# Weight tiles grouped 2, 1, 4 and 3, parameter vectors on SyncE's queue, and one transposing load for each of B and C

## The chip, the cores and the metric

The kernel runs on one core of one Trainium2 chip. The metric is device time in microseconds (us), from the start to the end of one execution. A profile is one further execution, taken by the hardware profiler; its span runs from the first to the last instruction of the program.

## What is computed

A layer norm over 2048 rows of 512 features, and then the sum of three things: the input itself, a diagonal state-space model (SSM), and a gated feed-forward block. The state matrix B has 512 states by 512 features, C has 512 features by 512 states, and the feed-forward block is 1376 wide.

```python
xn = layernorm(x)                                   # (1, 2048, 512)
# A: state-space model, one complex state per p
Lam_bar = exp(exp(log_dt) * (Lambda_re + 1j * Lambda_im))
B_bar = ((Lam_bar - 1.0) / Lam)[:, None] * (B_re + 1j * B_im)
Bu = einsum("bld,pd->blp", xn, B_bar)
h[t] = Lam_bar * h[t - 1] + Bu[:, t]                # over 2048 steps
yA = 2.0 * einsum("blp,dp->bld", h, C).real + xn * Dskip
# B: feed-forward block
yB = (silu(xn @ w_gate) * (xn @ w_up)) @ w_down     # width 1376
out = x + yA + yB
```

All inputs are bfloat16.

## The kernel before

The 2048 rows are worked through in four chunks of 512 rows, each of four tiles of 128 rows. `xall` holds the input by row tiles, `xnT` the normalised rows transposed (features on the partitions). The feed-forward width is cut into eleven feature tiles `fi`: ten of 128 and one of 96.

The order of all work is written out by hand. TensorE (PE) carries the matmuls: gate and up products of a feature tile (`gu_mm`, L425: four matmuls of 512 columns for gate and four for up), the products with B (`bproj_tile`, L350: `part` 0 is the real half, `part` 1 the imaginary half; for each part four state tiles `q`, each of four matmuls over the feature blocks `k`), the down product (L505) and the product with C (L514). ScalarE (ACT) empties the accumulators, VectorE (DVE) does the norms and the SSM's scan, GpSimd (POOL) a few small operations and the stores of results that are added to the output.

The head is finer. While the first chunk's rows arrive tile by tile, `head_mm` (L597) multiplies each row tile as it comes with the first three feature tiles (`H = 3`, `fi` 0 to 2), gate (`which` 0) and up (1). `xT_pe(n)` (L213) transposes row tile `n` on PE; with tile 2 it also transposes the twelve parameter rows `prm_rows` (L243), from which DVE and ACT make the SSM's constants. After the head the order on PE is: gate and up of `fi` 3 to 6 (`G0 = 7`), B with chunk 0 (`part` 0, then `part` 1), gate and up of `fi` 7 to 9, the last feature tile, B with chunk 1, and so on.

The loads that feed this go out on three queues, in the order in which the code names them:

- SyncE (SP): `xall` tile 0, gate weights of group 0, `xall` tile 2, gate and up weights of group 1 (L130, L131), the second chunk's rows in two loads of two tiles (L136), gate and up of group 2 (L137, L138), B's real half in four transposing loads (L141), gate and up of group 3, B's imaginary half in four transposing loads, the last feature tile's weights (L146, L147), then the transposes of chunk 1's normalised rows (`xT_dma`, L227), what `load_late` brings, and C in eight transposing loads (L714).
- ACT: `xall` tile 1, up weights of group 0, `xall` tile 3.
- POOL: the three parameter vectors (L134), 1 KB each, ahead of the identity matrix that PE's transposes need and of an index ramp.

A group is a run of feature tiles that one load brings for gate and one for up, given by `fgroups`: (0, 2), (2, 4), (4, 7), (7, 10) before. A load's line in the profile is L112, the body of `load_w1`.

In the built program, loads from SP and ACT take eight semaphores in turn, and a load is issued only when the load that last used its semaphore, the eighth before it in the order of the code, has landed. A reader of the data waits on the same semaphore, so it waits for a whole load: for one block `k` of B with four loads, for a whole half of B with one.

Of the kernel before, what the change touches and what calls it, by code (L numbers as in the profile page):

```python
# [23 lines left out]
def kernel(  # L24
# [17 lines left out]
    nc = tc.nc  # L42
# [8 lines left out]
    TPC = CW // 128  # L51
    KD = D // 128
    NQ = Pst // 128
    FT = (F + 127) // 128
# [24 lines left out]
    x_v = A_x[0].rearrange("(n p) d -> p n d", p=128)  # L79
# [5 lines left out]
    xall = const.tile([128, NT, D], BF16, name="xall")  # L85
    xnT = const.tile([128, KD, L], BF16, name="xnT")

    fgroups = [(0, 2), (2, 4), (4, 7), (7, FT - 1)]
    wg_g, wu_g = [], []
    for gi, (a, b) in enumerate(fgroups):  # L90
        cols = min(F, b * 128) - a * 128
# [5 lines left out]
    BT = const.tile([128, 2, KD, Pst], BF16, name="BT")  # L97
    CT = const.tile([128, 2, NQ, D], BF16, name="CT")
# [11 lines left out]
    def load_w1(q, tiles, view, gi):  # L110
        a, b = fgroups[gi]
        q.dma_start(out=tiles[gi][:], in_=view[:, :, a * 128:min(F, b * 128)])  # L112
# [18 lines left out]
    load_w1(nc.sync, wu_g, wu_v, 1)  # L131
    prm_rows = const.tile([3 * NQ, 128], BF16, name="prm_rows")
    for i, v in enumerate((A_Lambda_re, A_Lambda_im, A_log_dt)):
        nc.gpsimd.dma_start(out=prm_rows[i * NQ:(i + 1) * NQ, :], in_=v.rearrange("(q j) -> q j", j=128))  # L134
    for n in (TPC, TPC + 2):
        nc.sync.dma_start(out=xall[:, n:n + 2, :], in_=x_v[:, n:n + 2, :])  # L136
    load_w1(nc.sync, wg_g, wg_v, 2)  # L137
    load_w1(nc.sync, wu_g, wu_v, 2)  # L138
    for part, src in enumerate((A_B_re, A_B_im)):
        for k in range(KD):  # L140
            nc.sync.dma_start_transpose(out=BT[:, part, k, :], in_=src[:, k * 128:(k + 1) * 128])  # L141
        if part == 0:
            load_w1(nc.sync, wg_g, wg_v, 3)
            load_w1(nc.sync, wu_g, wu_v, 3)
# [565 lines left out]
        pump(GU)  # L710
        multiply(1)
    for part, src in enumerate((A_C_re, A_C_im)):
        for q in range(NQ):
            nc.sync.dma_start_transpose(out=CT[:, part, q, :], in_=src[:, q * 128:(q + 1) * 128])  # L714

    bproj_chunk(1)
    fwd1, back1 = ssm_ops(1)
# [52 lines left out]
```

## Time and profile before

| | |
|---|---|
| median of 3 runs | 179.78 us (179.59 to 179.90) |
| the profiled execution | 179.83 us |
| its span | 178.1 us |
| outside the span | 1.7 us |
| PE busy | 173.7 us, 98% of the span |
| DVE, ACT, POOL busy | 153.3, 94.2, 23.2 us |
| granted clock of PE | 0.999 |

The span in 40 slices of 4.45 us, busy share in tenths:

```profile
PE   7899999999999999999999999999999999999993
DVE  3789997999999999999999999999999999940033
ACT  3579696978499966033997660024866610220000
DMA  5998956994236400021920000007286900073012
GB/s 159 327 254 204 144 98 174 361 184 104 44 76 218 180 0 0 0 29 14 137 61 0 0 0 0 4 0 81 29 125 84 156 2 0 0 79 39 4 48 70
```

A digit is the busy share of one slice, 9 for 90% or more; for DMA it is the mean of the core's 16 DMA engines, and the last row is what they moved. PE is at 9 from the third slice to the last but one. The DMA engines are full in the second to fourth slice (4.5 to 18 us), when the first weights, the second chunk's rows and B come in.

### The profile page before, as it was taken

To read this page: it belongs to the slowest core of one execution; us is meant where nothing else is said; L and a number is where in the kernel's file an instruction comes from. 1 tells how busy PE (TensorE), PEld (TensorE's weight loads), DVE (VectorE), ACT (ScalarE), POOL (GpSimd) and SP (SyncE) were. 2 spreads that over 40 slices of the span, in tenths; PEclk is the share of its full clock that TensorE was granted. 3 is DMA by queue.
4 is the path that set the end of the run, shared out by engine and by line. 5 is a ranking of instruction groups with operands and counts; after the bars stand their busy time and mean duration, and the time that the engine had idled before them with its cause. 6 is when DMAs were issued, how large, how long until landed. Compare 5 with 4: busy or idle time off the path is not lost.

```text
span 178.1 us, 2462 instructions
## 1 busy us (share of the span) xinstructions
PE 173.7 (98%) x916; PEld 83.2 (47%) x916; DVE 153.3 (86%) x233; ACT 94.2 (53%) x173; POOL 23.2 (13%) x29
## 2 busy tenths in 40 slices
PE   7899999999999999999999999999999999999993
PEld 2784444444444444444444444444444444444743
DVE  3789997999999999999999999999999999940033
ACT  3579696978499966033997660024866610220000
POOL 6003000001400000029100000013405000150000
PEclk9999999999999999999999999999999999999999
DMA  5998956994236400021920000007286900073012
GB/s 159 327 254 204 144 98 174 361 184 104 44 76 218 180 0 0 0 29 14 137 61 0 0 0 0 4 0 81 29 125 84 156 2 0 0 79 39 4 48 70
DMA packets 29131, 15.53 MB, mean 87 GB/s; under 512 B 17824, under 2 KB 29056, under 8 KB 29088
## 3 DMA queue, kind: packets, MB, share of 16 engines
q1 hardware_dynamic: 24416, 11.41, 28.9%
q0 software_dynamic: 3456, 3.28, 14.5%
q10 hardware_dynamic: 1248, 0.69, 1.4%
q8 instruction: 7, 0.11, 0.3%
q14 instruction: 4, 0.03, 0.1%
HBM read 8.03 MB, written 5.24 MB: 75 GB/s over the span
## 4 chain that ended last, share of the span: by engine, by line
PE 96%; DMA 1%; DVE 1%; issue 0%
PE ps L425 36%; PE ps L505 21%; PE ps L514 16%; PE ps L350 16%; PE ps L597 3%; PE ps L451 2%; DMA xall<-in_A_x_dram 1%; PE ps L461 1%; PE ps L213 1%; DVE stats L178 0%; DVE stats L604 0%; DVE xall L196 0%; DVE res L517 0%; PE ps L574 0%; DVE mv L179 0%
## 5 line engine op out<-in xcount | busy, mean ns | idle before, releaser
L505 PE MATMUL ps<-wd_sb,guT 128*128 128x512 bf16 (+3 forms) x198 | 38.8, 355 | 0.0
L425 PE MATMUL ps<-xnT,wg 128*128 128x512 bf16 x148 | 38.0, 379 | 0.0
L425 PE MATMUL ps<-xnT,wu 128*128 128x512 bf16 x148 | 38.0, 379 | 0.0
L392 DVE TENSOR_TENSOR_SCAN g<-r_t,car,u 128x512 bf16<-128x512 f32 x24 | 28.9, 1265 | 0.0
L514 PE MATMUL ps<-CF,wt 128*128 128x512 bf16 (+2 forms) x144 | 28.3, 355 | 0.0
L350 PE MATMUL ps<-xnT,BT 128*128 128x512 bf16 x128 | 28.3, 379 | 0.0
L505 PEld LDWEIGHTS <-guT 128*128 128x128 bf16 (+1 forms) x198 | 18.5, 98 | 19.9
L521 ACT CAST res<-ps 128x512 bf16<-128x512 f32 x12 | 7.0, 585 | 38.5 <-PE ps L514 38.5
L439 ACT ACTIVATE guT<-ps 128x512 bf16<-128x512 f32 x40 | 24.8, 619 | 3.9 <-PE ps L425 3.7
L440 ACT CAST u<-ps 128x512 bf16<-128x512 f32 x40 | 24.2, 604 | 4.2 <-PE ps L425 4.2
L425 PEld LDWEIGHTS <-wu 128*128 128x128 bf16 x148 | 14.5, 98 | 17.5
L425 PEld LDWEIGHTS <-wg 128*128 128x128 bf16 x148 | 14.3, 98 | 17.6 <-issue 0.8
L522 POOL DMA_DIRECT2D out_dram<-res x12 | 11.1, 997 | 87.2 <-ACT res L521 87.2
L514 PEld LDWEIGHTS <-wt 128*128 128x128 bf16 x144 | 13.4, 98 | 14.3
L350 PEld LDWEIGHTS <-BT 128*128 128x128 bf16 x128 | 12.5, 98 | 15.1
L352 ACT CAST u<-ps 128x512 bf16<-128x512 f32 x32 | 17.5, 589 | 3.1 <-PE ps L350 3.1
L517 DVE TENSOR_TENSOR res<-ps,xn_end 128x512 bf16<-128x512 f32 (+2 forms) x6 | 3.0, 514 | 14.6 <-PE ps L514 14.6
L444 DVE TENSOR_TENSOR guT<-guT,u 128x1024 bf16<-128x1024 bf16 x20 | 13.5, 680 | 0.0
L178 DVE BATCH_NORM_STATS2 stats<-xall 128x6 f32<-128x512 bf16 x14 | 9.4, 670 | 1.9 <-DMA xall<-in_A_x_dram 1.9
L360 DVE TENSOR_TENSOR pm<-u,c 128x2048 bf16<-128x2048 bf16 x8 | 9.8, 1220 | 1.2 <-ACT c L277 1.1
L188 POOL TENSOR_TENSOR rstd<-ve,neg_half 128x4 f32<-128x4 f32 x3 | 5.3, 1750 | 40.7 <-DVE ve L187 40.7
L360 DVE TENSOR_TENSOR pm<-g,c 128x2048 bf16<-128x2048 bf16 x8 | 9.7, 1218 | 0.1
(103 smaller groups left out, 156.9 us busy)
## 6 DMA issues: line engine op xcount, KB each, us to landing
out_dram<-in_A_x_dram SPq DMA_DIRECT2D x1, 1536.0 KB, 8.0
out_dram<-res POOLq DMA_DIRECT2D x12, 128.0 KB, 3.2
out_dram<-xall POOLq DMA_DIRECT2D x3, 512.0 KB, 5.9
wd_sb<-in_B_w_down_dram SPq DMA_DIRECT2D x1, 1280.0 KB, 10.6
xall<-in_A_x_dram SPq DMA_DIRECT2D x1, 1024.0 KB, 5.9
wg<-in_B_w_gate_dram SPq DMA_DIRECT2D x2, 384.0 KB, 5.4
wu<-in_B_w_up_dram SPq DMA_DIRECT2D x2, 384.0 KB, 6.0
wg<-in_B_w_gate_dram SPq DMA_DIRECT2D x2, 256.0 KB, 4.5
```

The lines of the kernel that those rows point to most:

```text
L178: nc.vector.bn_stats(out=stats[:, n, :], in_=xall[:, n, :])
L350: nc.tensor.matmul(ps[:], lhsT=BT[:, part, k, q * 128:(q + 1) * 128], rhs=xnT[:, k, c * CW:(c + 1) * CW], start=(k == 0), stop=(k == KD - 1))
L352: nc.scalar.copy(out=u_tiles[c][:, part, q, :], in_=ps[:])
L360: V.tensor_tensor(out=t[:], in0=flat(src()[:, i]), in1=flat(tab[:]), op=ALU.mult)
L392: V.tensor_tensor_scan(out=g()[:, part, q, :], data0=r_t[:, q:q + 1].to_broadcast([128, CW]), data1=u_tiles[c][:, part, q, :], initial=ini ...
L425: nc.tensor.matmul(ps[:fs, lo:hi], lhsT=wslice(groups, fi, k), rhs=xnT[:, k, c * CW + lo:c * CW + hi], start=(k == 0), stop=(k == KD - 1))
L439: nc.scalar.activation(out=guT[:fs, fi, :], in_=psg[:fs], func=ACT.Silu)
L440: nc.scalar.copy(out=u_pair[c][:fs, fi % 2, :], in_=psu[:fs])
L444: products.append(lambda: V.tensor_tensor(out=g, in0=g, in1=u, op=ALU.mult))
L505: nc.tensor.matmul(o[:], lhsT=gu_tiles[c][:fsz[fi], fi, i * 128:(i + 1) * 128], rhs=wd_sb[:fsz[fi], fi, lo:hi], start=(fi == 0), stop=False)
L514: nc.tensor.matmul(o[:], lhsT=w_tiles[c][:, part, q, i * 128:(i + 1) * 128], rhs=CF[:, part, q, lo:hi], start=False, stop=(part == 1 and q ...
L522: nc.gpsimd.dma_start(out=out_v[:, n, lo:hi], in_=res[:, lo:hi], accum_op=ALU.add)
```

## The change

Four edits, all of loads; no arithmetic changes.

```diff
-    fgroups = [(0, 2), (2, 4), (4, 7), (7, FT - 1)]
+    fgroups = [(0, 2), (2, 3), (3, 7), (7, FT - 1)]
...
     for i, v in enumerate((A_Lambda_re, A_Lambda_im, A_log_dt)):
-        nc.gpsimd.dma_start(out=prm_rows[i * NQ:(i + 1) * NQ, :], in_=v.rearrange("(q j) -> q j", j=128))
-    for n in (TPC, TPC + 2):
-        nc.sync.dma_start(out=xall[:, n:n + 2, :], in_=x_v[:, n:n + 2, :])
+        nc.sync.dma_start(out=prm_rows[i * NQ:(i + 1) * NQ, :], in_=v.rearrange("(q j) -> q j", j=128))
+    for a, b in ((0, 1), (1, 2), (2, 4)):
+        nc.sync.dma_start(out=xall[:, TPC + a:TPC + b, :], in_=x_v[:, TPC + a:TPC + b, :])
     load_w1(nc.sync, wg_g, wg_v, 2)
     load_w1(nc.sync, wu_g, wu_v, 2)
     for part, src in enumerate((A_B_re, A_B_im)):
-        for k in range(KD):
-            nc.sync.dma_start_transpose(out=BT[:, part, k, :], in_=src[:, k * 128:(k + 1) * 128])
+        nc.sync.dma_start_transpose(out=BT[:, part, :, :], in_=src[:, :])
...
     for part, src in enumerate((A_C_re, A_C_im)):
-        for q in range(NQ):
-            nc.sync.dma_start_transpose(out=CT[:, part, q, :], in_=src[:, q * 128:(q + 1) * 128])
+        nc.sync.dma_start_transpose(out=CT[:, part, :, :], in_=src[:, :])
```

Group 1 shrinks from two feature tiles to one (256 KB to 128 KB for gate, the same for up), and group 2 grows from three to four (384 KB to 512 KB each): feature tile 3 moves from group 1 to group 2. The three parameter loads stand on SP behind the up weights of group 1. The second chunk's rows come in loads of one, one and two tiles. Each half of B and of C, 512 KB, comes in one transposing load in place of four of 128 KB. SP then issues four transposing loads of B and C in place of sixteen, three parameter loads and one row load more; its order is otherwise the same, and the instructions of PE, DVE and ACT stand in the same order as before.

## Prediction, on record before the changed kernel ran

> **What bounds the kernel now.** I read the chain of waits first (it says which engine sets the end), then the waits of TensorE (PE), then the weight loads of PE in the head, SyncE's (SP's) queue in time order, and last the loads of short windows with their time to landing.
>
> The chain of waits, by engine, and the list of everything PE waited for:
>
> ```profile
> PE 96%; DMA 1%; DVE 1%; issue 0%
> PE ps L574 <- PEq L754: 0.8, 1, 0.8
> PE ps L213 <- DVE xall L196: 0.7, 1, 0.7
> ```
>
> From 4.96 us PE never waits as long as the view lists. So the end comes where the sum of PE's work puts it: a gain must come from small gaps in the head, and a load that comes late costs its lateness in full, because nothing later has slack to give back.
>
> The small gaps, in PE's weight loads (start, duration, in brackets the idle time before and what ended it):
>
> ```profile
> 7.44 0.27 PEld L597 LDWEIGHTS <-wu 128*128 128x128 bf16 x4
> 7.88 0.33 PEld L597 LDWEIGHTS <-wg 128*128 128x128 bf16 x4 [0.18 <-DMA wg<-in_B_w_gate_dram]
> 8.23 0.32 PEld L213 LDWEIGHTS <-xall 128*128 128x128 bf16 x4
> 8.65 0.09 PEld L243 LDWEIGHTS <-prm_rows 12*128 12x128 bf16 x1
> 8.78 0.33 PEld L597 LDWEIGHTS <-wu 128*128 128x128 bf16 x4
> 12.08 0.58 PEld L425 LDWEIGHTS <-wg 128*128 128x128 bf16 x4
> 12.78 0.53 PEld L425 LDWEIGHTS <-wu 128*128 128x128 bf16 x3
> ```
>
> At 7.88 the gate weights of feature tile 2 (group 1) come 0.17 us late: PE's matmuls stood 0.056 apart up to 7.66, and the next started at 7.89. At 8.78 the up weights (landed at 8.74) are up to 0.07 late. Feature tile 3 starts at 12.08 (gate) and needs its up weights at 12.78; tile 3 is what moves into the later, larger group.
>
> SP's issues (start, us):
>
> ```profile
> 2.20 0.43 SPq L112 DMA_DIRECT2D wg<-in_B_w_gate_dram  x1
> 2.67 0.51 SPq L112 DMA_DIRECT2D wu<-in_B_w_up_dram  x1
> 3.23 1.71 SPq L136 DMA_DIRECT2D xall<-in_A_x_dram  x2
> 4.98 0.47 SPq L112 DMA_DIRECT2D wg<-in_B_w_gate_dram  x1
> 5.81 0.87 SPq L112 DMA_DIRECT2D wu<-in_B_w_up_dram  x1
> 6.72 6.26 SPq L141 DMA_TRANSPOSE BT<-in_A_B_re_dram  x4
> 13.03 1.24 SPq L112 DMA_DIRECT2D wg<-in_B_w_gate_dram  x1
> 14.86 5.36 SPq L141 DMA_TRANSPOSE BT<-in_A_B_im_dram  x4
> ```
>
> A plain load costs SP about 0.5 us, a transposing one of 128 KB about 1.26. Adding the times to landing (5.6, 6.1, 6.3, 5.7, 6.4 and 6.8 us in the trace for group 1's gate and up, the two row loads, group 2's gate and up) gives landings at 7.84, 8.74, 9.49, 10.25, 11.43 and 12.62: in order of issue, each later than the one before by its own size. So the queue is the limit there, and prices are differences: 256 KB in 512-byte rows 0.90 us, 256 KB of x in 1024-byte rows 0.755, 384 KB in 768-byte rows 1.185. B's halves landed at 15.90 and 22.30 (last load of each: issue at 11.72 plus 4.2, at 18.96 plus 3.3); PE starts on B here:
>
> ```profile
> 19.04 7.07 PE L350 MATMUL ps<-xnT,BT 128*128 128x512 bf16 x32
> ```
>
> Sixteen of these 32 matmuls, 0.216 us apart, belong to the real half, so the imaginary half is first needed at 19.04 + 16 x 0.216 = 22.49.
>
> **The change part by part.**
>
> *Group 1 smaller.* Rows of 128 columns are 256 bytes, which no plain load of the trace has. Per row (32 on each of 16 DMA engines) the prices above are 28.1 ns for 512 bytes, 37.0 for 768 and 47.2 for 1024: a line with 9 ns at its foot, so 18.6 ns for 256 bytes and 0.60 us for a load. Bounds: 0.45 (half of 0.90) and 0.90. I take 0.60, as three rows lie on the line. Group 1's gate then lands at 7.84 - 0.30 = 7.54, its up weights at 8.14. PE wants them at 7.66 and 8.65 or sooner. The gain is 0.17 + 0.04 (half of the 0.07) = 0.21; bounds 0 and 0.35 (with the 0.10 that PE loses ahead of L243, whose cause the trace doesn't tell).
>
> *Parameters on SP.* POOL loses 0.69 + 0.56 + 0.52 us of issues; its identity matrix, done at 3.6, is first used at 4.96 after DVE, so this gives nothing. On SP the three issues (some 0.45 each) wait for the loads eight back, which landed at 2.96, 3.64 and 4.55; the next issue, x, must wait for group 0's up weights at 5.85 in any case, so these issues lie in a wait. The vectors land behind group 1's up weights, at about 8.2; PE needs them at 8.65 - 0.17 = 8.48. Cost 0, by 0.3 us of cover; beyond it each tenth costs a tenth, and DVE's and ACT's constants (L246 to L252) come as much later.
>
> *x in three.* Issues at 5.87, 6.3 and 6.8, landings 8.14 plus 0.38, 0.38 and 0.755: 8.52, 8.90, 9.65. DVE reads them from 11.59. Cost 0. The queue doesn't run dry: the first load of all took 2.2 us alone, so x could land at 8.1 at the earliest, before its turn.
>
> *Group 2 larger.* 512 KB in 1024-byte rows is 2 x 0.755 = 1.51 us. Gate may be issued when group 1's gate has landed (7.54) and lands at 9.65 + 1.51 = 11.16, up at 12.67. PE, 0.21 ahead, wants gate at 11.9 and up at 12.78 - 0.21 = 12.57 for loading ahead, or 12.74 at the latest for a matmul at 12.79. Cost 0, but the cover is 0.1 us: with 0.90 for each load of group 1 up lands at 13.27 and feature tile 3's up matmuls start at 13.32 in place of 13.00, 0.32 later than before.
>
> *B in one load each.* No row has a transposing load of 512 KB. Its issue is bounded by 1.25 us (one of the present ones) and by 7.95 (C's real half, four issues in a full queue, 30.89 to 38.84); between lie 5.0 (4 x 1.26), 5.36 and 6.26. I take 5.0: the work per byte is the same. SP gets to the real half when group 2's up issue is over, at 8.15 + 0.87 = 9.0 (before: 6.72). Real half issued until 14.0, group 3's two loads until 15.0, imaginary half until 20.0. Landing follows the end of an issue by 1.2 us (transposes of chunk 1's rows: 2.4 to landing with 1.22 of issue) to 2.1 (last load of the imaginary half, 3.35 - 1.26). So the real half lands by about 16.1, needed at 18.6; the imaginary half at 21.2 to 22.1. It is needed whole at 22.49 - 0.21 = 22.28, where before the first matmul needed a quarter of it. Cost 0, cover 0.2 to 1.1 us. Behind these on SP are the last tile's weights (needed at 31.3), chunk 1's transposes (issued at 21.51 before, about 21.2 now; needed at 32.15, landed by 27.95) and the late loads: cover of 4 us and more. Group 3 is needed at 25.7 and lands before 20.
>
> A rule bears on this: the Trainium skill, "Advanced Engine Details and Errata", section "X-Bar Transpose (TRN2)", says that transposing DMAs on this chip are as fast as regular ones. The trace disagrees: 1.26 us of SP against 0.5, and 3.3 us from 12.62 to 15.90 for 512 KB. By the rule the imaginary half would land long before it is needed, the sum would be the same, and the first rival below would be gone.
>
> *C in one load each.* First read by ACT at 58.8, landed by 45.5 before: 13 us of cover, cost 0.
>
> *Sum* against the profiled execution: 179.83 - 0.21 = 179.6 us, which is 0.1% under the median of the runs shown (179.78).
>
> **The rivals.**
>
> 1. *The imaginary half of B comes late (slower).* The real half takes 6.26 us of SP again, group 3's gate 1.24, the imaginary half 5.36: 9.0 + 6.26 + 1.24 + 0.6 + 5.36 = 22.5, landing at 23.7 to 24.5. PE then stands 1.4 to 2.3 us at `part` 1, net +1.2 to +2.1: about 181.4. It decides from a landing after 22.3. For it: the cover is thin, SP starts B 2.3 us later, and the present issues did take so long. Against: 1.1 of the 6.26 fell in the first load, at 6.72, with a queue that is shorter by 9.0.
> 2. *The up weights of feature tile 3 come late*: 0.90 for a load of group 1, +0.32: 180.15. Against: three row sizes lie on one line. With a landing 0.1 later still it passes 0.2%.
> 3. *Both of PE's head gaps and the 0.10 ahead of L243 vanish*: -0.35, 179.48.
> 4. *The large transposing load works like four*: then B lands as before and only the head counts; this is within the forecast.
>
> **How the numbers follow.** 0.2% (0.36 us) is about what a measurement of this kernel can tell from no change. Forecast, -0.35 to +0.2 us: 0.50. Rival 1: 0.33, nearly all of it slower. Rival 2: 0.12, half of it over 0.2%. Rival 3 or more: 0.05. A gain over 0.36 us has no gap in PE that could pay for it, so faster gets 0.07, for what I haven't seen; slower 0.33 + 0.06 = 0.39 with rounding up to 0.41; same 0.52. The likeliest time is 179.6. The range runs from 179.4 (rival 3 less 0.1 of scatter between runs) to 181.4 (the middle of rival 1); the forecast's own range is 179.45 to 180.05.
>
> **What would show it.** Right: no PEld wait on a DMA at 7.7 to 8.8; feature tile 3's up weights loaded without a gap at about 12.6; 32 L350 matmuls in 6.9 to 7.1 us without a wait; the chain still 96% PE. Wrong: a PE wait on `wu` near 12.8 or on `BT` near 18.6 or 22.3, or one on `prm_rows` near 8.5; an issue of a transposing load far from 5.0 us.

## The result, and the profile after

The changed kernel takes 180.68 us (median of 7 executions, 180.21 to 181.10) against 179.78 (7 executions, 179.59 to 180.02): ratio 1.0052, 95% interval 1.0035 to 1.0068. It is 0.9 us slower where no change was forecast. The profiled execution took 180.64 us: 178.57 of span and 2.07 outside it, against 178.05 and 1.78.

The chain of waits of the changed kernel, by engine, and further down some of its pieces in order of time (start, duration, what). Lines of code have moved up by one or two:

```profile
PE 91%; DMA 6%; SPq 1%; issue 0%; DVE 0%
```

```profile
6.95 0.43 SPq L136
...
7.42 0.47 SPq L112
...
7.93 5.60 DMA wu<-in_B_w_up_dram
13.53 0.05 issue
13.58 6.22 PE ps L424 x28
19.80 6.91 PE ps L349 x32
```

Before, the chain was 96% PE and 1% DMA. Now it runs over SP's issues to one load, the up weights of group 2, and from 13.58 us on it is PE alone. What PE waited for (total, times, longest):

```profile
PE ps L573 <- PEq L752: 0.8, 1, 0.8
PE ps L424 <- DMA wu<-in_B_w_up_dram: 0.4, 1, 0.4
PE ps L212 <- DVE xall L195: 0.2, 1, 0.2
```

The middle line is new. Its place, in PE's weight loads:

```profile
7.80 0.37 PEld L596 LDWEIGHTS <-wg 128*128 128x128 bf16 x4
8.19 0.32 PEld L212 LDWEIGHTS <-xall 128*128 128x128 bf16 x4
8.61 0.09 PEld L242 LDWEIGHTS <-prm_rows 12*128 12x128 bf16 x1
8.72 0.33 PEld L596 LDWEIGHTS <-wu 128*128 128x128 bf16 x4
...
12.09 0.55 PEld L424 LDWEIGHTS <-wg 128*128 128x128 bf16 x4
13.58 0.55 PEld L424 LDWEIGHTS <-wu 128*128 128x128 bf16 x4 [0.94 <-DMA wu<-in_B_w_up_dram]
```

The gap at feature tile 2's gate weights, 0.18 before, is gone at 7.80. At feature tile 3 the weight loads stand idle for 0.94 us until the up weights have landed. The matmuls there, before and after:

```profile
12.13 1.03 PE L425 MATMUL ps<-xnT,wg 128*128 128x512 bf16 x4
13.00 1.03 PE L425 MATMUL ps<-xnT,wu 128*128 128x512 bf16 x4
```

```profile
12.10 1.04 PE L424 MATMUL ps<-xnT,wg 128*128 128x512 bf16 x4
13.58 1.04 PE L424 MATMUL ps<-xnT,wu 128*128 128x512 bf16 x4 [0.45 <-DMA wu<-in_B_w_up_dram]
```

The up matmuls follow the gate matmuls by 1.48 us in place of 0.87. So the wait holds PE up by 0.61 us (the 0.45 in brackets is shorter because the ends of overlapping matmuls are modelled), and of the gap that was closed only 0.03 us of lead was left here. The up matmuls start 0.58 us later than before; B starts at 19.64 (before 19.04), and the last matmul of all at 175.60 (before 175.01). The +0.58 at 13 us is the +0.59 at the end: nothing later is late, and nothing later gives back. B itself takes what it took:

```profile
19.64 7.07 PE L349 MATMUL ps<-xnT,BT 128*128 128x512 bf16 x32
```

SP's queue shows where the lateness comes from:

```profile
2.68 0.51 SPq L112 DMA_DIRECT2D wu<-in_B_w_up_dram  x1
3.23 0.44 SPq L134 DMA_DIRECT2D prm_rows<-in_A_Lambda_re_dram  x1
4.30 0.26 SPq L134 DMA_DIRECT2D prm_rows<-in_A_Lambda_im_dram  x1
4.60 0.29 SPq L134 DMA_DIRECT2D prm_rows<-in_A_log_dt_dram  x1
6.06 1.31 SPq L136 DMA_DIRECT2D xall<-in_A_x_dram  x3
7.42 0.47 SPq L112 DMA_DIRECT2D wg<-in_B_w_gate_dram  x1
7.93 0.51 SPq L112 DMA_DIRECT2D wu<-in_B_w_up_dram  x1
8.48 4.96 SPq L140 DMA_TRANSPOSE BT<-in_A_B_re_dram  x1
```

The parameter loads have taken three semaphore turns. The rows that were issued at 3.23 are issued from 6.06, and group 2 at 7.42 and 7.93 in place of 4.98 and 5.81. Meanwhile the loads that were in flight land (group 1 at 6.92 and 7.26), and the DMA engines have nothing to do. The changed kernel's windows (stretch, length, busy times with counts, granted clock, DMA share, GB/s):

```profile
5.50:6.50 1.00, 1.00 (x18) 1.00 (x16) 0.92 (x3) 0.41 (x2) 0.00 (x0) 1.00 1.16 266
6.50:7.25 0.75, 0.75 (x17) 0.73 (x14) 0.72 (x3) 0.71 (x3) 0.00 (x0) 1.00 0.08 13
7.25:8.50 1.25, 1.25 (x22) 1.21 (x19) 0.81 (x3) 0.63 (x3) 0.00 (x0) 1.00 0.87 270
8.50:10.00 1.50, 1.50 (x24) 1.33 (x22) 1.12 (x6) 0.42 (x3) 0.00 (x0) 1.00 0.95 244
10.00:11.50 1.50, 1.50 (x31) 1.50 (x28) 1.24 (x9) 1.47 (x2) 0.00 (x0) 1.00 1.03 343
```

For 0.75 us they move 13 GB/s, then 244 to 270 until 10 us, and only then 343. In the kernel before the same stretches were full:

```profile
6.50:7.25 0.75, 0.75 (x16) 0.73 (x14) 0.71 (x3) 0.74 (x3) 0.00 (x0) 1.00 1.12 300
7.25:8.50 1.25, 1.24 (x19) 1.02 (x17) 0.76 (x3) 0.62 (x3) 0.00 (x0) 1.00 1.12 347
8.50:10.00 1.50, 1.50 (x23) 1.31 (x21) 1.08 (x6) 0.28 (x2) 0.00 (x0) 1.00 1.09 332
```

Group 2's up weights land at 13.53; before, with loads a quarter smaller, at 12.62, when feature tile 3 did not yet depend on them.

Outside the span the changed kernel takes 2.08 us (median of its executions) against 1.79 in the kernel before. That is the other part of the loss.

### The profile page after: what moved, and what is told of

Its sections match the earlier page's. It is cut to its first block, busy times and chain, and to the rows that moved or that the text cites. A ratio compares the mean times of both kernels' runs of the same rounds, so it can differ in the third digit from the quotient of the medians.

```text
span 178.6 us, 2437 instructions
## 1 busy us (share of the span) xinstructions
PE 174.4 (98%) x916; PEld 83.4 (47%) x916; DVE 153.2 (86%) x233; ACT 95.2 (53%) x173; POOL 21.4 (12%) x26
## 4 chain that ended last, share of the span: by engine, by line
PE 91%; DMA 6%; SPq 1%; issue 0%; DVE 0%
PE ps L424 36%; PE ps L504 21%; PE ps L513 16%; PE ps L349 15%; DMA wu<-in_B_w_up_dram 3%; DMA wg<-in_B_w_gate_dram 3%; PE ps L450 2%; PE ps L460 1%; SPq L112 0%; SPq L128 0%; SPq L136 0%; SPq L123 0%; DVE res L516 0%
```

## The experiments

For each run the kernel before was run on the same chip beside it (for e1 to e14 15 to 27 executions, medians of 179.69 to 179.90 us, of the span 177.9 to 178.1). "SP" is the number of loads and stores that SP issues, "up lands" the landing of group 2's up weights, "gap" PE's idle time in front of feature tile 3's up matmuls as the profile shows it, "tail" from the last matmul's start to the span's end; these four are from the profiled execution. Span and outside are medians over the executions.

| run | SP | up lands | gap | tail | span | outside | ratio to before, interval |
|---|---|---|---|---|---|---|---|
| before | 50 | 12.62 | 0 | 3.04 | 178.0 | 1.79 | |
| after | 42 | 13.53 | 0.45 | 2.96 | 178.6 | 2.08 | 1.0052 [1.0035, 1.0068] |
| e1 | 39 | 12.29 | 0 | 3.20 | 178.15 | 1.81 | 1.0004 [0.9993, 1.0014] |
| e2 | 42 | 12.97 | 0 | 2.96 | 178.2 | 2.01 | 1.0017 [1.0007, 1.0027] |
| e3 | 54 | 13.47 | 0.35 | 3.74 | 179.65 | 1.78 | 1.0084 [1.0059, 1.0109] |
| e4 | 53 | 12.44 | 0 | 3.85 | 178.85 | 1.79 | 1.0044 [1.0027, 1.0061] |
| e5 | 42 | 11.43 | 0 | 2.97 | 178.0 | 2.08 | 1.0016 [1.0006, 1.0025] |
| e6 | 41 | 13.45 | 0.27 | 3.05 | 178.9 | 1.94 | 1.0064 [1.0042, 1.0087] |
| e7 | 50 | 12.27 | 0 | 2.99 | 177.9 | 1.77 | 0.9998 [0.9988, 1.0008] |
| e8 | 42 | 13.03 | 0 | 2.92 | 178.35 | 2.06 | 1.0043 [1.0028, 1.0058] |
| e9 | 50 | 12.68 | 0 | 3.04 | 178.2 | 1.78 | 1.0007 [0.9999, 1.0016] |
| e10 | 38 | 12.45 | 0 | 3.27 | 178.15 | 1.80 | 1.0012 [1.0003, 1.0021] |
| e11 | 50 | 13.53 | 0.19 | 3.03 | 179.0 | 1.77 | 1.0066 [1.0037, 1.0095] |
| e12 | 42 | 12.35 | 0 | 3.00 | 177.95 | 2.19 | 1.0022 [1.0011, 1.0033] |
| e13 | 47 | 12.76 | 0 | 3.17 | 178.25 | 1.79 | 1.0016 [1.0007, 1.0025] |
| e14 | 50 | 11.43 | 0 | 3.06 | 178.0 | 1.77 | 1.0001 [0.9992, 1.0010] |

Theory A: the parameter loads' three semaphore turns delay the rows and group 2, the queue runs empty, and the up weights of feature tile 3, which the new groups have put into the later load, come late. Its rivals put the wait down to the size of group 2's loads (theory B), or to the single transposing loads (theory C).

**e1: the parameters back on POOL**, all the rest of the change kept.

```diff
-        nc.sync.dma_start(out=prm_rows[i * NQ:(i + 1) * NQ, :], in_=v.rearrange("(q j) -> q j", j=128))
+        nc.gpsimd.dma_start(out=prm_rows[i * NQ:(i + 1) * NQ, :], in_=v.rearrange("(q j) -> q j", j=128))
```

> The changed kernel with the parameter loads back on POOL. Theory A (semaphore turns): the three parameter loads and the extra row load push the second chunk's rows and group 2 four turns back, so they are issued at 6.06 and later in place of 3.23, the DMA engines stand idle from 6.5 to 7.25 us, and feature tile 3's up weights land at 13.53. Without the parameter loads x goes out at 3.2 again, up lands by 12.7, PE's wait of 0.9 us at its weight load goes, and the span is 178.0 or less (0.5 to 0.6 below the changed kernel's 178.6). Theory B (size): the 512 KB group is late by itself; the wait at feature tile 3 stays at 0.4 us or more and the span at 178.5. Outside the span: 1.7 us (as before) if POOL's loads decide it, 2.05 (as changed) if they don't.

The rows and group 2 go out as soon as in the kernel before, and the wait is gone. SP's queue of this run, and then its windows:

```profile
3.22 2.27 SPq L136 DMA_DIRECT2D xall<-in_A_x_dram  x3
5.97 0.38 SPq L112 DMA_DIRECT2D wg<-in_B_w_gate_dram  x1
6.43 0.47 SPq L112 DMA_DIRECT2D wu<-in_B_w_up_dram  x1
```

```profile
6.50:7.25 0.75, 0.75 (x14) 0.75 (x13) 0.57 (x3) 0.27 (x1) 0.00 (x0) 1.00 1.17 274
7.25:8.50 1.25, 1.25 (x23) 1.21 (x21) 0.89 (x3) 0.78 (x4) 0.00 (x0) 1.00 1.10 338
8.50:10.00 1.50, 1.50 (x20) 1.30 (x19) 1.00 (x6) 0.51 (x3) 0.00 (x0) 1.00 1.07 343
```

The DMA engines are full where they stood still. With the same 512 KB loads of group 2 and the same single transposing loads, the up weights land 1.24 us sooner (12.29), and the time is that of the kernel before. (The span of this run's one profile, 178.6, is long for another reason, slow matmuls in the head, see the end; the median over the executions is 178.15.)

**e2: the old groups**, all the rest of the change kept.

```diff
-    fgroups = [(0, 2), (2, 3), (3, 7), (7, FT - 1)]
+    fgroups = [(0, 2), (2, 4), (4, 7), (7, FT - 1)]
```

> The changed kernel with the old groups 2, 2, 3, 3. Theory A and B alike: feature tile 3 lies in group 1 again and has landed by 9, so PE has no wait near 13; feature tile 4 needs group 2 at 13.65 and 14.5, where up lands at about 13.4. Span about 178.0 to 178.2. Theory C (the transposing loads slow the weights or B itself comes late): a wait stays, span 178.5. Outside the span: 2.05 if the groups have no part in it.

No wait either: group 2 is late here too (12.97), but feature tile 3 is in group 1. So the wait takes both edits. What is left of the ratio, 1.0017, is for the most part the time outside the span (2.01).

**e3: B and C in four transposing loads each again**, all the rest of the change kept.

```diff
-        nc.sync.dma_start_transpose(out=BT[:, part, :, :], in_=src[:, :])
+        for k in range(KD):
+            nc.sync.dma_start_transpose(out=BT[:, part, k, :], in_=src[:, k * 128:(k + 1) * 128])
```

(The same for C.)

> The changed kernel with four transposing loads for each half of B and of C. Theory A and B: nothing changes for feature tile 3, its up weights land at about 13.5 and the span stays at 178.4 to 178.8. Theory C (the one long issue from 8.48 us slows the 1024-byte packets of group 2, which took 0.2 to 0.7 us each at 8.4 to 9.8): group 2 lands 0.5 us or more earlier, span 178.1. Outside the span: 1.7 if the number of transposing loads decides it, else 2.05.

The up weights land at 13.47, the wait stays: theory C, by which B's single load holds them up, falls. (Its expectation reads slow packets off the changed kernel's trace; they are a few among many, see the next part.) The run is slower still, because the tail behind the last matmul grew to 3.74 us.

**e4: the parameters on SP alone**, the kernel before otherwise.

```diff
-        nc.gpsimd.dma_start(out=prm_rows[i * NQ:(i + 1) * NQ, :], in_=v.rearrange("(q j) -> q j", j=128))
+        nc.sync.dma_start(out=prm_rows[i * NQ:(i + 1) * NQ, :], in_=v.rearrange("(q j) -> q j", j=128))
```

> The kernel before with only the parameter loads moved to SP. Theory A: x goes out at about 6 in place of 3.23 and group 2 about 2 us later, but feature tile 3 lies in group 1, so PE waits little: span within 0.2 of 178.1. If the parameters came late PE would wait at L243 near 8.6. Outside the span: 2.05 if moving POOL's loads decides it, else 1.7.

No wait at feature tile 3, and the last matmul starts at 174.89, a little earlier than before. The whole loss is in the tail: 3.85 us in place of 3.04. It is not what slows the changed kernel, whose tail is 2.96; e9 and e10 ask for its cause.

**e5: group 2 ahead of the second chunk's rows**, in the changed kernel.

```diff
+    load_w1(nc.sync, wg_g, wg_v, 2)
+    load_w1(nc.sync, wu_g, wu_v, 2)
     for a, b in ((0, 1), (1, 2), (2, 4)):
         nc.sync.dma_start(out=xall[:, TPC + a:TPC + b, :], in_=x_v[:, TPC + a:TPC + b, :])
-    load_w1(nc.sync, wg_g, wg_v, 2)
-    load_w1(nc.sync, wu_g, wu_v, 2)
```

> The changed kernel with the two loads of group 2 issued ahead of the three of the second chunk's rows. Theory A (the up weights of feature tile 3 come late because the parameter loads take three semaphore turns, so that SP issues the rows and group 2 at 6.06 to 8.4 us in place of 3.2 to 6.7, and the DMA engines stand nearly idle from 6.5 to 7.25): group 2 is issued at about 6.0 and 6.5, its up weights land at 10.5 to 11.5 us instead of 13.53, PE has no wait on them at feature tile 3, and the span's median comes down from 178.6 to 178.0 to 178.2; with the 2.05 us outside the span, which nothing here should change, 180.1 to 180.3. Rival (the load of four feature tiles is itself slow): a wait on the up weights stays, and so does 180.6.

As theory A has it. SP's queue of this run, and its weight loads at feature tile 3:

```profile
4.75 0.29 SPq L134 DMA_DIRECT2D prm_rows<-in_A_log_dt_dram  x1
5.93 0.39 SPq L112 DMA_DIRECT2D wg<-in_B_w_gate_dram  x1
6.37 0.51 SPq L112 DMA_DIRECT2D wu<-in_B_w_up_dram  x1
7.10 1.52 SPq L138 DMA_DIRECT2D xall<-in_A_x_dram  x3
```

```profile
12.14 0.59 PEld L424 LDWEIGHTS <-wg 128*128 128x128 bf16 x4
12.84 0.74 PEld L424 LDWEIGHTS <-wu 128*128 128x128 bf16 x4
```

The queue still runs empty (44 GB/s from 6.50 to 7.25), but what goes out first is now what PE wants first. The span is back at 178.0; the 2.08 outside stays.

**e6: the rows in two loads**, in the changed kernel: one turn fewer.

```diff
-    for a, b in ((0, 1), (1, 2), (2, 4)):
-        nc.sync.dma_start(out=xall[:, TPC + a:TPC + b, :], in_=x_v[:, TPC + a:TPC + b, :])
+    for n in (TPC, TPC + 2):
+        nc.sync.dma_start(out=xall[:, n:n + 2, :], in_=x_v[:, n:n + 2, :])
```

> The changed kernel with the second chunk's rows in two loads of two tiles, as before: one semaphore turn fewer in front of group 2. Theory A: gate of group 2 waits for one load less and is issued about 0.5 us earlier, the up weights land at about 13.0 in place of 13.53, PE's wait there shrinks from 0.6 to about 0.1 us: span about 178.1 to 178.3. If the three row loads cost nothing, as predicted, the landing stays at 13.5 and the span at 178.6.

A miss for my expectation. Group 2's loads are issued 0.5 to 0.6 us earlier (6.90 and 7.32), as expected, and yet the up weights land at 13.45, not 13.0. So it isn't the issue of the last load that sets the landing. Nor is it the point at which the queue starts again: the first rows were issued at 5.69 here and at 6.06 in the changed kernel, and all rows had landed at 9.22 and at 9.66, but here the gate weights took 2.84 us behind them. What counted was how slowly the engines then worked: from 8.50 to 10.00 they moved 219 GB/s (244 in the changed kernel). The third row load costs nothing, as predicted.

**e7: the new groups alone**, in the kernel before.

```diff
-    fgroups = [(0, 2), (2, 4), (4, 7), (7, FT - 1)]
+    fgroups = [(0, 2), (2, 3), (3, 7), (7, FT - 1)]
```

> The kernel before with the new groups alone: parameters stay on POOL, rows in two loads, B and C in four loads for each half. The prediction's own terms: the wait of 0.17 us at feature tile 2's gate weights goes, group 2's up weights land at about 12.5 to 12.7, with no wait on them: span 0.1 to 0.25 us under the 178.1 of the kernel before, nothing changed outside it, 179.6 to 179.75. Rival (group 2 with four tiles is too big to land in time in any arrangement): a wait on the up weights near 12.8 and 180.0 or more.

With a full queue 512 KB are no trouble: the up weights land at 12.27, and PE doesn't wait. Its weight loads at feature tile 2:

```profile
7.54 0.27 PEld L597 LDWEIGHTS <-wu 128*128 128x128 bf16 x4
7.76 0.37 PEld L597 LDWEIGHTS <-wg 128*128 128x128 bf16 x4
8.68 0.33 PEld L597 LDWEIGHTS <-wu 128*128 128x128 bf16 x4
```

No idle time stands in brackets: the gap of 0.18 is closed. The last matmul of the profiled execution starts 0.105 us earlier than before (174.904 against 175.009), but over the executions the gain can't be told from none (0.9998).

**e8: three tiny memsets on POOL** in place of its three issues, in the changed kernel, for the time outside the span.

```diff
+    pad = const.tile([128, 4], F32, name="pad")
+    for i in range(3):
+        nc.gpsimd.memset(pad[:, i:i + 1], 0.0)
```

> The changed kernel with three tiny memsets added on POOL, in the place where its three parameter issues were, so that POOL's program has about its old length. For the 0.25 us more that the changed kernel takes outside its span: if they hang on POOL's program being three instructions shorter, they go, 2.05 becomes 1.8, and the time is about 180.4; if not, 2.05 and 180.65 stay. The span (178.6) and the wait on the up weights at feature tile 3 stay in both cases.

Outside the span nothing moved: 2.06. In this profiled execution the up weights came at 13.03 and PE happened not to wait, since its head ran late (feature tile 3's gate matmuls started at 12.46, in the changed kernel at 12.10); the span's median is still 178.35, against 177.9 for the kernel before in the same comparison.

**e9: the parameters on SP, and C's real half in one load**, in the kernel before. Three loads more, three fewer: the stores at the end get the old semaphore turns. Beside e4's edit:

```diff
     for part, src in enumerate((A_C_re, A_C_im)):
+        if part == 0:
+            nc.sync.dma_start_transpose(out=CT[:, part, :, :], in_=src[:, :])
+            continue
         for q in range(NQ):
```

> The kernel before with two edits: the parameter loads on SP's queue, and C's real half in one transposing load in place of four. Three loads more and three less, so the loads behind them take the same semaphore turns as in the kernel before and in the changed kernel. Against the run with the parameters on SP alone, whose last matmul started at 174.9 us but whose last store and end waits took 3.85 us behind it: if that tail hangs on the turns that the final stores get, it is back at 2.9 to 3.1 and the span at 177.9 to 178.0; if on the parameters' queue, 3.8 stays and 178.8. Feature tile 3 is in group 1, so PE has no wait on its up weights. Outside the span: 2.05 if the parameters on SP alone cause the 0.25 more (and the long tail hid it), 1.8 if it takes the large transposing load of B too. In all 179.7 to 180.0 by the turns, 180.6 by the queue.

The tail is 3.04 again: e4's loss hung on the turns, not on the queue that carries the parameters. Outside: 1.78, so the parameters on SP alone don't cause the 0.28. New is a gap of 0.2 us in front of the transpose of `prm_rows`, whose last vector landed at 8.56: with group 1 at its old size the parameters can be late (also in e13, at 8.75; in e4 they landed at 8.43, and PE didn't wait).

**e10: B and C in one load for each half**, in the kernel before.

```diff
-        for k in range(KD):
-            nc.sync.dma_start_transpose(out=BT[:, part, k, :], in_=src[:, k * 128:(k + 1) * 128])
+        nc.sync.dma_start_transpose(out=BT[:, part, :, :], in_=src[:, :])
...
-        for q in range(NQ):
-            nc.sync.dma_start_transpose(out=CT[:, part, q, :], in_=src[:, q * 128:(q + 1) * 128])
+        nc.sync.dma_start_transpose(out=CT[:, part, :, :], in_=src[:, :])
```

> The kernel before with B and C in one transposing load for each half, nothing else. Twelve loads fewer, so the final stores get other semaphore turns, those of the run with four transposing loads for each half and all the rest of the change. If the turns set the tail, it is 3.6 to 3.9 us from the last matmul's start and the span 178.6 to 178.9; if the parameters on SP do, 3.0 and 177.9 to 178.1. No wait on B or C in PE (the prediction's cost of 0 for both): last matmul at 174.8 to 175.2. Outside the span 1.8 if the parameters on SP are needed for more. Theory A: group 2 is issued from 5.0 us on and lands by 12.5, no PE wait.

PE waits for neither B nor C. The tail is 3.27, between the two expectations: with twelve loads fewer the final stores take the same turns as in e3 (four loads more; turns go by eights), where it was 3.74. So the turns move the tail but are not all of it.

**e11: the new groups and the parameters on SP**, in the kernel before, with C's real half in one load to keep the turns: the diffs of e4, e7 and e9 together.

> The kernel before with three edits: the new groups, the parameters on SP, and C's real half in one load so that the semaphore turns stay; second chunk's rows in two loads and B in four for each half, as before. Theory A: these two of the change's edits are enough, group 2's up weights land at 13.0 to 13.6 us, PE waits 0.2 to 0.6 us at feature tile 3, the last matmul starts at 175.2 to 175.6, the span is 178.2 to 178.6. Rival (it takes B's single load, which shares the DMA engines, or the third row load): up lands before 12.9, no wait, 177.9. Outside the span as in the run with the parameters on SP and C's half alone.

These two edits are enough. Weight loads of this run at feature tile 3:

```profile
12.31 0.58 PEld L425 LDWEIGHTS <-wg 128*128 128x128 bf16 x4
13.57 0.33 PEld L425 LDWEIGHTS <-wu 128*128 128x128 bf16 x3 [0.68 <-DMA wu<-in_B_w_up_dram]
```

The landing is the changed kernel's (13.53), with the rows in two loads and B in fours. The span's median, 179.0, is even above the 178.2 to 178.6 I expected; the executions run from 178.4 to 180.9.

**e12: B in one load for each half and C's real half in two**, in the kernel before: 42 loads and stores on SP, as in the changed kernel, with the parameters on POOL. **e13: the parameters on SP and B in one load for each half**: 47, the diff of e4 and the first half of e10's. In e12, beside B's:

```diff
     for part, src in enumerate((A_C_re, A_C_im)):
+        if part == 0:
+            for q in (0, 2):
+                nc.sync.dma_start_transpose(out=CT[:, part, q:q + 2, :], in_=src[:, q * 128:(q + 2) * 128])
+            continue
         for q in range(NQ):
```

> For the 0.25 us more outside the span. In the runs so far it goes with the number of loads and stores that SP issues: 38 and 39 give 1.80, 41 gives 1.94, 42 gives 2.01 to 2.08, 50 to 54 give 1.78; but the runs with 41 and 42 are also those that have both the parameters on SP and B and C in single loads. This is the kernel before with B in one transposing load for each half and C's real half in two: 42 on SP, parameters on POOL. If the number counts: 2.0 to 2.1 outside, about 180.1 in all. If the two edits together do it: 1.8 and 179.8. In both cases no PE wait and a span of 177.9 to 178.2.

> The kernel before with the parameters on SP and B in one load for each half, C as before: 47 loads and stores on SP. If parameters on SP together with B's single loads cause the 0.25 us outside the span: 2.05. If the number of SP's loads and stores does, and its window ends between 42 and 47: 1.8. Feature tile 3 is in group 1, so no PE wait on its up weights; the final stores get other turns than before, so the tail may be 3.0 to 3.9 us.

e12 takes 2.19 outside the span (2.08 to 2.25 in nine of its twelve executions, 1.72 to 1.79 in three), e13 takes 1.79. So the pair of edits isn't what it takes: the parameters can be on POOL. All runs with 41 or 42 loads and stores on SP have 1.94 to 2.19, all with 38, 39 or 47 to 54 have 1.77 to 1.81. That is an order in the runs, and not yet a cause; the mechanism is open.

**e14: both causes undone.** The changed kernel with group 2 first (as in e5), B in two loads for each half and C in four: 50 on SP again. Groups, parameters on SP and rows in three loads are kept. Beside e5's diff:

```diff
-        nc.sync.dma_start_transpose(out=BT[:, part, :, :], in_=src[:, :])
+        for k in (0, 2):
+            nc.sync.dma_start_transpose(out=BT[:, part, k:k + 2, :], in_=src[:, k * 128:(k + 2) * 128])
...
-        nc.sync.dma_start_transpose(out=CT[:, part, :, :], in_=src[:, :])
+        for q in range(NQ):
+            nc.sync.dma_start_transpose(out=CT[:, part, q, :], in_=src[:, q * 128:(q + 1) * 128])
```

> The changed kernel with both causes undone, and the groups, the parameters on SP and the rows in three loads kept: group 2 issued ahead of the second chunk's rows, B in two transposing loads for each half and C in four, so that SP again issues 50 loads and stores and the final stores get the turns of the kernel before. If the wait on the up weights and the number of SP's loads and stores are all that the change costs: no PE wait, last matmul at 174.8 to 175.1 us, tail 3.0, span 177.8 to 178.1, 1.8 outside, 179.6 to 179.9, the same as before. If something else of the change costs: 180.1 or more.

179.77 us against 179.74 for the kernel before, ratio 1.0001: no wait on the weights, 1.77 outside. With both undone nothing of the loss is left that these runs could tell (the interval is 0.1% wide on either side). No arrangement tried beats the kernel before.

## Why the prediction was wrong

The loss of 0.9 us has two parts: 0.58 us in the span and 0.28 us outside it. The range that I gave, 179.4 to 181.4, holds 180.68 by luck alone: its upper part was there for rival 1, a late imaginary half of B, which did not come about.

**The step that failed** is the landing of group 2: "Gate may be issued when group 1's gate has landed (7.54) and lands at 9.65 + 1.51 = 11.16, up at 12.67." The issue was right (7.42), the landing of the rows was right (9.66, forecast 9.65), and the up weights followed the gate by 1.48, as priced. But the gate weights took 2.39 us behind the rows, not 1.51, so all came 0.86 to 0.89 us later than forecast. The 1.51 was read from a queue that is always full. How long group 2's gate, 512 KB, lands behind the last row load, and up behind gate, with what the engines moved from 6.50 to 7.25 us:

| run | GB/s, 6.50 to 7.25 | gate | up |
|---|---|---|---|
| e1 | 274 | 1.49 | 1.50 |
| e7 | 264 | 1.50 | 1.55 |
| after | 13 | 2.39 | 1.48 |
| e3 | 32 | 1.65 | 1.39 |
| e6 | 85 | 2.84 | 1.39 |
| e8 | 143 | 1.76 | 1.48 |
| e11 | 79 | 2.48 | 1.44 |

(In e3 the last rows were late as well, at 10.44; its gate landed at 12.09.) In a full queue the price holds to 0.02 us for gate and 0.04 for up. The premise that broke stands a paragraph earlier: "The queue doesn't run dry". I worked out that the rows could land no sooner than 8.1 and set this against their turn, behind group 1, which was due at 8.14. But group 1 landed at 7.26, and what followed was not served at the full rate.

An empty queue is not the whole of it. In e2, e4, e9 and e13, with the parameters on SP and the old groups, the engines still moved 249 to 293 GB/s from 6.50 to 7.25, and yet group 2's gate, there 384 KB, landed 1.71 to 2.05 us behind the rows (1.18 in the kernel before). All eleven runs with the parameters on SP share something else: of the packets of 512 bytes and more that started between 6.5 and 11 us, 7 to 35 took 0.2 us or longer (24 in the changed kernel; most take 0.03 to 0.05). The five with the parameters on POOL have 0 to 2. In the changed kernel these packets make about 0.4 us of sixteen engines' time (an estimate: 7.1 us of packets over 16), near half of the 0.88 by which gate was late. Why they are slow no run shows.

The same reasoning was owed to every load behind the rows: the first rows, 128 KB issued at 6.06, moved no data before about 7.25 (the window above: 13 GB/s up to there) and landed at 8.20. The Trainium skill, "DMA: Bandwidth & Descriptors", section "Anatomy of one DMA — SWDGE (gpsimd) path", which treats POOL's path, gives each transfer a fixed cost of about 2 us, most of it on completion. The 2.14 us from issue to landing agree with that total; but here, on SP's queue, 1.2 of them lie in front of the first data, so less than half is left for completion. By its fit a load of 128 KB takes 2.3 us, an estimate near the 2.14.

**Rival 2** named the place and the direction (up late, feature tile 3 waits), at 13.27 and +0.32, but by another cause, a dearer price for group 1. It named the place for a reason that did not hold: group 1 was in fact cheaper than forecast, not dearer. The chance of late up weights was put too low, since 0.1 us of cover stood against a price that had only been seen in a full queue.

**Group 1 smaller.** The gap closed, as forecast. The price of 0.60 us for a load with 256-byte rows was too high: with a full queue up landed 0.36 us behind gate in e7 (7.39 and 7.75), below my lower bound of 0.45, and 0.51 in e1. So group 1 was through sooner, and the queue ran empty sooner. The gain of 0.21 is shown neither by the medians of e7 (its interval allows 0.22 us of gain and 0.14 of loss) nor in the changed kernel, whose feature tile 3 started 0.03 us earlier.

**Parameters on SP.** Their issues lie in a wait and PE didn't wait for them (L242 at 8.61, no gap), as said. The cost I put at 0 is what they did to the loads behind: the move itself was followed, its effect on the queue's filling was not. Without the move (e1) the wait is gone; with nothing of the change but the move and the groups (e11) it is there.

**B and C.** SP's issue of 4.96 and 4.45 us for the halves of B stands against 5.0 predicted; the imaginary half landed at 22.15 (21.2 to 22.1) and was wanted at 19.64 + 16 x 0.216 = 23.09, so rival 1 fell; had PE not been 0.58 us late, 0.36 us of cover would have been left. The measurement keeps contradicting the rule weighed there, that transposing loads are as fast as regular ones (the Trainium skill, "Advanced Engine Details and Errata", section "X-Bar Transpose (TRN2)"): a plain load of the same 512 KB takes 0.5 us of SP, a transposing one the 4.96 and 4.45 above. C landed by 41.2 and cost nothing in PE.

**Outside the span** I had no term at all. The 0.28 us were not to be read from any view of the kernel before.

## What to carry to other kernels

A price per load read between landings held while the queue was full. Before using it, follow the queue's filling: when does the last load in flight land, when is the next issued, and does its first data come in time? Where that can't be answered from a trace, a cover of 0.1 us is no cover. An issue of 1 KB costs little by itself, but where loads take semaphores in turn it costs a turn, and everything behind it on that queue is held until an older load has landed; the order behind it should then be the order in which the data are wanted (e5).

## What the runs showed of the hardware

- Time outside the span went with the number of loads and stores that SP issues: 1.94 to 2.19 us with 41 or 42, 1.77 to 1.81 with 38, 39 and 47 to 54. e12 shows both values in one kernel. Its cause is open.
- The tail from the last matmul to the end was 2.9 to 3.9 us. At the end SP waits for eighteen semaphores in nine pairs; which of them the final stores hold depends on the number of loads ahead modulo eight, and e4 against e9 shows 0.8 us from it with the same queue for the parameters. e10 shows that it isn't the turn alone.
- With the parameters on SP, 7 to 35 DMA packets of 512 bytes and more between 6.5 and 11 us took 0.2 us or longer, with them on POOL 0 to 2. Its cause is open too.
- The matmuls of the head run slower at first, for a time that varies between executions: the transposes of row tile 0 at 4.9 to 5.2 us took 0.22 us in the profile before and up to 0.31 in the changed kernel's and in e1's, where matmuls are at 0.22 from 5.75 and 6.78 us on; the view's granted clock is 1.00 in all three. The Trainium skill, "TensorE: Matmul & The Clock Gate", section "Part 1: The HAM clock gate (the "warmup" mystery)", says that the warm-up goes by a free-running window of some 3.4 us, so that the number of cold matmuls varies from run to run; this agrees. It moves single profiles of this kernel by some tenths, as much as the edits here, so medians over executions decide.
